# From its third chunk on, the first block in pairs of fp16 with scales from g_norm and the weights; the second block's weights kept in SBUF

## The chip, the cores and the metric

The kernel runs on one core of a Trainium2 chip. The metric is the time on the device in microseconds, from launch to end. Three runs of the kernel before gave 1608.7 us as their median (1608.4 to 1612.33).

## The reference, cut to what matters

```python
kv  = einsum('bhsd,bhse->bhde', k, v)           # linear attention, 8 x 8 heads, 576 tokens, 64 wide
out = einsum('bhsd,bhde->bhse', q, kv)
x   = out / sqrt(mean(out**2, -1) + 1e-6) * g_norm   # -> 4608 tokens x 512
h   = x @ moe_w_in                              # first block: 512 -> 2048
x   = maximum(0.01 * h, h) @ moe_w_out          # 2048 -> 512
h   = x @ moe2_w_in                             # second block: 512 -> 2048
P   = a[0] + a[1]*h + a[2]*h**2 + a[3]*h**3
Q   = 1 + |b[0]|*|h| + |b[1]|*h**2
out = (P / (Q + 1e-6)) @ moe2_w_out             # 2048 -> 512
```

The weights arrive as fp64 words; the kernel narrows them to fp32 itself.

## The kernel before

The 4608 tokens are 9 chunks of 512 columns; the hidden width of 2048 is 16 tiles f of 128. Each matrix product of a block is made from pairs, a high part and the rest, in three matmuls: `mm3` (L294) multiplies low weight by high value, high by high and high by low into one PSUM tile. A chunk and a tile f take 12 matmuls of 128x128 by 512 columns into ph (`emit_h`, L302: the weights W[0,f]) and 12 into the four y tiles (`emit_y`, L308: W[1,f]); so 384 a chunk and block.

In the first block the pairs are of fp32r: weights in W (pool wp, tile `w{part}_{f}`, 4 KB a partition for high and low), x in X (`new_x`), g in `new_g`. In the second block they are of fp16: `split16` (L285) multiplies by a power of two, ScalarE writes the high part, VectorE the rest. The powers come from measured sizes: largest weights (`wst`), largest x2 values (`xst`).

The first block goes by units (L801): unit 0 and 1 are tiles 0 to 5 of chunks 0 and 1 and run inside a startup whose order is written out by hand (`STARTUP`), unit 2 and 3 are tiles 6 to 15 of chunks 0 and 1, units 4 to 10 are all tiles of chunks 2 to 8. One f of a unit is a slot (`sl`). A slot issues, in this order: loads, the 12 matmuls into ph, "early" steps, leaky on ScalarE (L554), the high part of g on ScalarE (L841), the low part on VectorE (L234), the 12 matmuls into y of the tile two slots back (LAG = 2), "pe" and "post" steps, and then weight work. The slots also carry the next chunk's attention (`prep`, L703), to whose results `sx` (L764) gives the form of pairs. The y tiles of a chunk are read out by `evac_y` (L327) and stored to DRAM as x2; chunks 0 and 1 pass through yp, since they are added up in two halves.

Unit 2 converts the rest of w1 (CONVERT, L804): in slot s the narrowing of two tiles on VectorE (L263 to L273), gl, and the rests of W[0, 8+s] and W[1, 6+s]; both are read from two slots on. Units 4 to 9 narrow w2 (three tiles f a unit), measure it and store it in fp32 to DRAM (w2f). Unit 10, the last, loads it back (`load_w2`, L793) and splits it into fp16 (`split_w2`, L289). `w2s`, `w2next` and `rest` carry this over the border into the second block.

The second block takes two tiles f at once (j, 8 to a chunk); ScalarE and VectorE work out the rational function, GpSimd the low half of g. The scales of chunk 8 are asked for in its chunk 0, at j = 3, and worked out at j = 4 (L981 to L984); `x_scales_ask` sends sums through DRAM, `x_scales` (L196) is a chain of small operations on VectorE and ScalarE.

Each engine works in its own order, as the program issues it; TensorE's order is the one above. All loads and stores but a few are on SP's queue, in order.

Of the kernel before, what the change touches and what calls it, by code (L numbers as in the profile page):

```python
# [48 lines left out]
def kernel(  # L49
# [40 lines left out]
    w2f = [dp.tile([P, 2, NC * P], F32, tag=f"w2_{f}", name=f"w2_{f}") for f in range(NF)]  # L90
# [9 lines left out]
    small = const.tile([P, 25 + 23 * NCH], F32, name="small")  # L100
# [8 lines left out]
    wst, wq, aba, b0a, sw, nw = (part_of_small(*x) for x in ((2, NC), (2, NC), (4,), (1,), (2,), (2,)))  # L109
    xst, xq = part_of_small(NCH, NC), part_of_small(NCH, NC)  # L110
# [12 lines left out]
    def set_constants(spread):  # L123
        nc.vector.memset(ones.bitcast(F32), 0.0)
        nc.vector.memset(ones[0:D, 0:D].bitcast(F32), 1.0 / D)
        nc.vector.memset(ones[D:P, D:P].bitcast(F32), 1.0 / D)
# [54 lines left out]
    def weight_scales(t):  # L181

        reduce(nw[:, 0:1], t[:, 0, :], ALU.add)
        reduce(nw[:, 1:2], t[:, 1, :], ALU.max)
        over_root(sw, nw)
        nc.vector.scalar_tensor_tensor(out=nw, in0=nw, scalar=MS_R, in1=sw, op0=ALU.mult, op1=ALU.mult)
        pow2_below(sw, sw)
        nc.vector.tensor_scalar_mul(sw, sw, TOP * MS_R)

# [99 lines left out]
    def split_w2(f, part, src):  # L289
        t = wp.tile([P, 4, NC * P], F16, tag=f"w{part}_{f}", name=f"v{part}_{f}")  # L290
        W[part, f] = (t[:, 0, :], t[:, 1, :])
        split16(*W[part, f], src, sw[:, part:part + 1])
# [9 lines left out]
    def emit_h(f, dst, xs):  # L302
        wh, wl = W[0, f]
# [4 lines left out]
    def emit_y(f, ys, gh, gl, first, last):  # L308
        wh, wl = W[1, f]
        for e in range(NC):  # L310
            mm3(ys[e], wh[:, e * P:(e + 1) * P], wl[:, e * P:(e + 1) * P], gh, gl, first, last)
# [15 lines left out]
    def evac_y(ys, dst, engines=(nc.scalar, nc.vector), part=None, to=None, x=None, scale=None):  # L327

        for i in range(NC // 2):
            t = part[i] if part else raw() if to is None else to[:, 2 * i:2 * i + 2, :]  # L330
            for j in range(2):
                src = ys[2 * i + j]
                if part:
                    nc.vector.tensor_tensor(out=t[:, j, :], in0=src, in1=t[:, j, :], op=ALU.add)
                elif scale is not None:
                    nc.scalar.activation(out=t[:, j, :], in_=src, func=AF.Copy, scale=scale)
# [24 lines left out]

    def split_x(c, cc, src):
        if cc == 0:
            t = [xp.tile([P, 2, N], F16, tag=f"xh{i}", name=f"x16_{i}") for i in range(NC)]
            X[NCH + c] = [[x[:, i, :] for x in t] for i in range(2)]
        split16(X[NCH + c][0][cc], X[NCH + c][1][cc], src, col["sx"][:, c:c + 1])

    with tc.manual_schedule():
        Y = {}
        G = {}  # L370
        with ExitStack() as actx:
# [180 lines left out]
            def leaky(ps):  # L552
                t = scratch("t", 3, "t")
                nc.scalar.activation(out=t, in_=ps, func=AF.Prelu, alpha=0.01)  # L554
                return t
# [137 lines left out]
            STEPS = {"tl": p_table, "c": lambda: set_constants(spread), "g": lambda: load_gain(gsc_row), "cg": p_gain, "mc": make_constants, "wu": p_warm,  # L693
# [9 lines left out]
            def prep(c, po_at, ms_at, w_at, x_at, bursts, joint=False):  # L703
# [60 lines left out]
                def sx(p):  # L764
                    if p == 0:
                        X[c] = new_x()
# [26 lines left out]
            def load_w2(parts):  # L793
                t = raw()
                for i, (f, part) in enumerate(parts):
                    nc.sync.dma_start(out=t[:, i, :], in_=w2f[f][:, part, :])
                return t

# [9 lines left out]
            w2n, w2next = [], None  # L808
# [4 lines left out]
            for ui, (c, f0, f1) in enumerate(units):  # L813
# [11 lines left out]
                for f in range(f0, f1):  # L825
# [4 lines left out]
                    w2s = w2n  # L830
                    w2n = [x for x in ((f, 0), (f - LAG, 1)) if 0 <= x[0]] if last else []
                    w2raw, w2next = w2next, load_w2(w2n) if w2n else None
# [17 lines left out]
                    for _ in range({2: 0, 3: 2}.get(sl, 1) if joint else len(pend) > LAG):  # L850
# [4 lines left out]
                        if pf == p1 - 1:  # L855
                            evac_y(Y.pop(pc), yp[pc] if p1 < NF else x2[pc], part=parts, to=squares() if joint else None,
                                   x=pc if p1 == NF else None)
# [5 lines left out]
                    if 3 < ui and not last:  # L863
                        for _ in range(({3: 1, 4: 1, 8: 1, 9: 1, 11: 1, 13: 1} if joint else {3: 1, 4: 1, 6: 1, 8: 1, 10: 1, 12: 1}).get(sl, 0)):
                            if conv2:
                                t, ui_, part = conv2.pop(0)
                                narrow_abs([t], ui_)
                                narrow([t], ui_)
                                reduce(wq[:, part, :], ui_[:, 0, :].bitcast(F32).rearrange("p (c n) -> p c n", c=NC), ALU.max, True)
                                nc.vector.tensor_tensor(out=wst[:, part, :], in0=wst[:, part, :], in1=wq[:, part, :], op=ALU.max)  # L870
                                if not conv2:
                                    stores.append((w2f[wf], u.bitcast(F32)))
                        if sl in ((2, 6, 9) if joint else (2, 5, 8)) and todo:
                            wf = todo.pop()
                            u = cvp.tile([P, 2, N], U32, tag="cv", name="cv")
                            conv2 = [(load_w64(w2, wf, i, raw(1, I64)[:, 0, :]), u[:, i:i + 1, :], i) for i in range(2)]
                    if ui == len(units) - 2 and sl == 9:
                        asked = weight_scales_ask()
                    if ui == len(units) - 2 and sl == 11:
# [8 lines left out]
                    for i, (wf, part) in enumerate(w2s):  # L888
                        split_w2(wf, part, w2raw[:, i, :])
# [30 lines left out]
        rest = []  # L920

        def emit_y2():
# [3 lines left out]
            emit_y(pf, Y[pc], *pg, pf == p0, pf == p1 - 1)  # L926
# [3 lines left out]
            if pc < NCH:  # L930
                evac_y(ys, x2[pc], (nc.scalar, nc.scalar), x=pc)
            elif pc < 2 * NCH - 1:
                evac_y(ys, out[pc - NCH].rearrange("e p n -> p e n"), scale=col["y"][:, pc - NCH:pc - NCH + 1])
# [12 lines left out]
        for c in range(NCH):  # L946
            kc = NCH + c
            for j in range(NP):
                ph = ps_h2.tile([P, 2, N], F32, tag="h2", name="ph2")
                gt = new_g16()  # L950
                if c == NCH - 1 and j == NP - 1:
                    split(*prev)
                    done = None
                    for i in range(2):
                        if i:
                            ph = ps_h2.tile([P, 2, N], F32, tag="h2", name="ph2")
                        emit_h(2 * j + i, ph[:, i, :], X[kc])
# [5 lines left out]
                else:  # L963
                    for i in range(2):
                        emit_h(2 * j + i, ph[:, i, :], X[kc])
# [8 lines left out]
                for f, part, t in rest:  # L974
                    split_w2(f, part, t)
                rest = []
                if c == 0 and j < 2:
                    fs = w2n if j == 0 else [(NF - 2, 1), (NF - 1, 1)]
                    t = w2next if j == 0 else load_w2(fs)
                    rest = [(f, part, t[:, i, :]) for i, (f, part) in enumerate(fs)]  # L980
# [51 lines left out]
```

## Time and profile before

| | |
|---|---|
| runs, median | 1608.7 us (1608.4 to 1612.33) |
| profiled execution | 1609.07 us, of which the span in the trace is 1607.3 us |
| TensorE busy | 1596.7 us, 99% |
| VectorE busy | 978.3 us, 61% |
| ScalarE busy | 823.2 us, 51% |
| chain that ended last | TensorE 96%, DMA 2%, ScalarE 1% |

The profile is of one execution. Times in it are microseconds from the span's start unless marked ns; PE is TensorE's matmuls, PEld its weight loads (which overlap), DVE VectorE, ACT ScalarE, POOL GpSimd, SP the queue of transfers. Matmuls are pipelined: one lasts longer than the distance to the next, so their rate is read from what happens at equal places in a loop.

### The profile page before, as it was taken

The page shows a single profiled execution, that of the slowest core. Times are in us where ns is not written, and L with a number is a line of the kernel's source. Part 1 is how long each engine was busy: PE and PEld are TensorE (multiplying, and loading weights), DVE is VectorE, ACT ScalarE, POOL GpSimd, SP SyncE. Part 2 cuts the span into 40 slices and gives each one's busy share as a digit, 9 for nine tenths or more (in the row PEclk, how much of TensorE's full clock was granted, in tenths as well). Part 3 has the DMA queues.
Part 4 walks back from the last instruction along what each step waited for, and adds up shares of the span by engine and source line. Part 5 has one row for each costly group of instructions (what it writes and reads, how often), then busy time and mean ns, then how long its engine had stood idle before and what let it go on. Part 6 is the DMA issues. An engine that isn't in the chain of part 4 may idle for free.

```text
span 1607.3 us, 19258 instructions
## 1 busy us (share of the span) xinstructions
PE 1596.7 (99%) x7904; PEld 1020.5 (63%) x7904; DVE 978.3 (61%) x1240; ACT 823.2 (51%) x1074; POOL 151.9 (9%) x74
## 2 busy tenths in 40 slices
PE   8999999999999999999999999999999999999999
PEld 5888778888888888878885444444444444444444
DVE  6786244434454444442367877777777777777776
ACT  6554333323333232332366666666666666666665
POOL 0000000000000000000001222212222222112221
PEclk9999999999999999999999999999999999999999
DMA  8454634342434333121241010101000010101000
GB/s 315 125 182 150 174 103 132 94 143 72 139 94 129 119 92 109 42 85 30 87 162 66 2 53 0 53 0 44 10 27 27 4 49 1 53 0 53 1 27 27
DMA packets 45660, 123.61 MB, mean 77 GB/s; under 512 B 6148, under 2 KB 6660, under 8 KB 45572
## 3 DMA queue, kind: packets, MB, share of 16 engines
q1 hardware_dynamic: 43248, 118.06, 22.9%
q10 hardware_dynamic: 2324, 4.33, 1.1%
q8 instruction: 62, 1.02, 0.3%
q14 instruction: 26, 0.21, 0.0%
HBM read 90.90 MB, written 31.46 MB: 76 GB/s over the span
## 4 chain that ended last, share of the span: by engine, by line
PE 96%; DMA 2%; ACT 1%; DVE 0%; issue 0%; SPq 0%; DVEq 0%
PE ph L295 16%; PE y L297 16%; PE ph L297 16%; PE ph L296 16%; PE y L295 16%; PE y L296 16%; PE kvacc L406 1%; DMA raw<-in_kv_dram 1%; PE po L423 1%; PE pm L623 1%; DMA dqx<-small 0%; DMA raw<-dqx 0%; PE po L436 0%; ACT p L905 0%; ACT z L911 0%; PE bc L642 0%
## 5 line engine op out<-in xcount | busy, mean ns | idle before, releaser
L234 DVE TENSOR_TENSOR gl<-t,gh 128x512 fp32r<-128x512 f32 x144 | 99.4, 691 | 338.5 <-ACT gh L841 326.1
L234 POOL TENSOR_TENSOR gl<-p,gh 128x1024 f16<-128x1024 f32 x70 | 151.7, 2166 | 1431.8 <-PE y L297 865.1
L554 ACT ACTIVATE t<-ph 128x512 f32<-128x512 f32 x144 | 85.7, 595 | 353.3 <-PE ph L297 352.9
L295 PE MATMUL ph<-xh,w 128*128 128x512 f32 x576 | 226.8, 394 | 0.0
L295 PE MATMUL y<-gh,w 128*128 128x512 f32 x576 | 224.4, 390 | 0.0
L296 PE MATMUL ph<-xh,w 128*128 128x512 f32 x576 | 224.3, 389 | 0.0
L297 PE MATMUL ph<-xl,w 128*128 128x512 f32 x576 | 224.3, 389 | 0.0
L297 PE MATMUL y<-gl,w 128*128 128x512 f32 x576 | 224.2, 389 | 0.0
L296 PE MATMUL y<-gh,w 128*128 128x512 f32 x576 | 224.1, 389 | 0.0
L297 PE MATMUL y<-gl,v 128*128 128x512 f16 x576 | 218.3, 379 | 1.7 <-POOL gl L234 1.7
L295 PE MATMUL y<-gh,v 128*128 128x512 f16 x576 | 218.3, 379 | 0.3 <-ACT gh L239 0.3
L295 PE MATMUL ph<-x,v 128*128 128x512 f16 x576 | 218.3, 379 | 0.0
L296 PE MATMUL ph<-x,v 128*128 128x512 f16 x576 | 218.3, 379 | 0.0
L297 PE MATMUL ph<-x,v 128*128 128x512 f16 x576 | 218.3, 379 | 0.0
L296 PE MATMUL y<-gh,v 128*128 128x512 f16 x576 | 218.3, 379 | 0.0
L295 PEld LDWEIGHTS <-v 128*128 128x128 f16 x1152 | 112.7, 98 | 138.1 <-issue 2.5
L903 ACT ACTIVATE e<-ph,small 128x1024 f32<-128x1024 f32 (+1 forms) x73 | 80.3, 1101 | 233.0 <-PE ph L297 233.0
L296 PEld LDWEIGHTS <-v 128*128 128x128 f16 x1152 | 112.7, 98 | 136.1 <-issue 0.6
L297 PEld LDWEIGHTS <-v 128*128 128x128 f16 x1152 | 112.7, 98 | 135.9
L906 DVE SCALAR_TENSOR_TENSOR e<-s,b,e 128x1024 f32<-128x1024 f32 (+1 forms) x73 | 92.7, 1270 | 148.0 <-ACT s L904 148.0
L295 PEld LDWEIGHTS ph<-xh,w 128*128 128x128 f32 x576 | 108.1, 188 | 29.2 <-issue 4.7
L295 PEld LDWEIGHTS y<-gh,w 128*128 128x128 f32 x576 | 108.1, 188 | 23.1 <-ACT tmp L258 0.4
(139 smaller groups left out, 2059.9 us busy)
## 6 DMA issues: line engine op xcount, KB each, us to landing
raw<-in_kv_dram SPq DMA_DIRECT2D x33, 512.0 KB, 5.8
tmp<-in_w_dram SPq DMA_DIRECT2D x32, 512.0 KB, 7.1
raw<-in_w_dram SPq DMA_DIRECT2D x32, 512.0 KB, 5.6
raw<-x SPq DMA_DIRECT2D x18, 512.0 KB, 5.5
w<-cv SPq DMA_DIRECT2D x16, 512.0 KB, 2.9
raw<-w SPq DMA_DIRECT2D x32, 256.0 KB, 3.6
out_dram<-raw SPq DMA_DIRECT2D x16, 512.0 KB, 2.9
raw<-in_qT_dram SPq DMA_DIRECT2D x28, 256.0 KB, 4.7
```

The source lines that it names most:

```text
L234: (nc.gpsimd if pool else nc.vector).tensor_tensor(out=lo, in0=src, in1=hi if hi.dtype == F16 else hi.bitcast(F32), op=ALU.subtract)
L295: nc.tensor.matmul(out=dst, lhsT=wl, rhs=xh, start=first, stop=False, **kw)
L296: nc.tensor.matmul(out=dst, lhsT=wh, rhs=xh, start=False, stop=False, **kw)
L297: nc.tensor.matmul(out=dst, lhsT=wh, rhs=xl, start=False, stop=last, **kw)
L406: nc.tensor.matmul(out=acc[s * D:(s + 1) * D, k * D:(k + 1) * D], lhsT=t[:, 0, c], rhs=t[:, 1, c], start=first and k == 0, stop=last, skip ...
L423: nc.tensor.matmul(out=dst[s][j * D:(j + 1) * D, o], lhsT=KV[bt][r, 2 * g + j, :], rhs=q[r, j, o], start=True, stop=True)
L554: nc.scalar.activation(out=t, in_=ps, func=AF.Prelu, alpha=0.01)
L623: nc.tensor.matmul(out=dst[32 * p:32 * (p + 1)], lhsT=pick, rhs=x, start=True, stop=True)
L903: nc.scalar.activation(out=e, in_=ph, func=AF.Abs, scale=k["e"])
L906: nc.vector.scalar_tensor_tensor(out=e, in0=s, scalar=b1[:, 0:1], in1=e, op0=ALU.mult, op1=ALU.add)
```

## The change

- Chunks 2 to 8 of the first block use fp16 pairs. In slots 5 to 9 of unit 3 and 0 to 9 of unit 4, `narrower` rewrites the 32 fp32r weight pairs as fp16 pairs (one ScalarE pass, two VectorE passes each), half the size, into places freed by the tile before. x gets the scale sx1, g the scale sg1 (in leaky's activation), y the scale sy1 in `evac_y`.
- The scales come from g_norm (`gain_scales`, at the end of the startup, with `gn` made in `p_gain`), and from the largest weights: `first_weight_top` on each of the 32 high parts, one a slot in unit 2, up to six a slot in unit 3, slots 0 to 3. `first_weight_norms` follows at slot 3, at slot 4 a matmul with the all-ones matrix adds over the partitions, and `first_scales` works the scales out.
- w2 is narrowed into tiles of wp that are free (V, in units 5 to 8, four f a unit in place of three in units 4 to 9), not stored to DRAM, and split in the last unit from there (W2).
- `weight_scales_ask` moves from slot 9 to 10, `weight_scales` from 11 to 13. Chunk 8's `x_scales_ask` and `x_scales` move from j = 3 and 4 of the second block's chunk 0 to j = 3 and 6 of its chunk 1.

```diff
-    w2f = [dp.tile([P, 2, NC * P], F32, tag=f"w2_{f}", name=f"w2_{f}") for f in range(NF)]
...
+    def gain_scales():
+
+        nc.vector.tensor_scalar(out=pgain, in0=gn, scalar1=2.0 ** -40, scalar2=None, op0=ALU.max)
+        pow2_below(pgain, pgain)
+        nc.vector.tensor_copy(out=sx1, in_=pgain)
+        one_over(sx1)
+        nc.vector.tensor_scalar_mul(sx1, sx1, 2.0 ** 11)
+        nc.vector.memset(m1, 0.0)
+
+    def first_weight_top(f, part):
+        reduce(wq[:, part, :], W[part, f][0].bitcast(F32).rearrange("p (c n) -> p c n", c=NC), ALU.max, True)
+        nc.vector.tensor_tensor(out=m1[:, part, :], in0=m1[:, part, :], in1=wq[:, part, :], op=ALU.max)
+
+    def first_weight_norms():
+        nc.vector.tensor_scalar(out=m1[:, 0, :], in0=m1[:, 0, :], scalar1=pgain, scalar2=None, op0=ALU.mult)
+        nc.vector.tensor_tensor(out=m1, in0=m1, in1=m1, op=ALU.mult)
+        reduce(nw1, m1, ALU.add)
+
+    def first_scales(ps):
+
+        over_root(sw1, ps)
...
+        over_root(sg1, nw1[:, 0:1])
+        nc.scalar.activation(out=sg1, in_=sg1, func=AF.Square, scale=MS_R)
...
+    order1 = [(p, k) for k in range(NF // 2) for p in range(2)]
+    order2 = [(p, k) for k in range(NF // 2, NF) for p in range(2)]
+    new_tiles, V, W2 = {}, {}, {}
+
+    def narrower(f, part):
+
+        if f not in new_tiles:
+            if f:
+                p, k = order1[f - 1]
+                t = wp.tile([P, 4, NC * P], F16, tag=f"w{p}_{k}", name=f"n_{f}")
+                new_tiles[f] = t[:, 0:2, :], t[:, 2:4, :]
+            else:
+                new_tiles[f] = [xp.tile([P, 2, NC * P], F16, tag=f"xl{i}", name=f"n_0{i}") for i in range(2)]
+        (wh, wl), t, s = W[part, f], new_tiles[f][part], sv1[:, part:part + 1]
+        hi, lo = t[:, 0, :], t[:, 1, :]
+        nc.scalar.activation(out=hi, in_=wh.bitcast(F32), func=AF.Copy, scale=s)
+        nc.vector.scalar_tensor_tensor(out=lo, in0=wh.bitcast(F32), scalar=s, in1=hi, op0=ALU.mult, op1=ALU.subtract)
+        nc.vector.scalar_tensor_tensor(out=lo, in0=wl.bitcast(F32), scalar=s, in1=lo, op0=ALU.mult, op1=ALU.add)
+        W[part, f] = hi, lo
...
+                nc.scalar.activation(out=gn, in_=t[:, 0:1], func=AF.Abs)
...
-                    split(X[c][0][p], X[c][1][p], x)
+                    split16(X[c][0][p], X[c][1][p], x, sx1)
...
-                        G[c, f // 2] = new_g()
+                        G[c, f // 2] = new_g16() if c > 1 else new_g()
...
-                    t = leaky(ph)
+                    t = leaky(ph, sg1) if c > 1 else leaky(ph)
...
+                    for _ in range(1 if ui == 2 else 6 if ui == 3 else 0):
+                        if top_of:
+                            first_weight_top(*top_of.pop(0))
+                    if ui == 3 and sl == 3:
+                        assert not top_of
+                        first_weight_norms()
+                    if ui == 3 and sl == 4:
+                        norms = bank("h", "norms")
+                        nc.tensor.matmul(out=norms[:, 0:2], lhsT=ones.bitcast(F32), rhs=nw1, start=True, stop=True)
+                        first_scales(norms[:, 0:2])
+                    for _ in range((3 if sl in (6, 7) else 2) if ui == 3 and sl > 4 else 2 if ui == 4 else 0):
+                        if wide and (ui > 3 or wide[0][0] < HALF):
+                            narrower(*wide.pop(0))
-                    if 3 < ui and not last:
...
+                    if 4 < ui and not last:
+                        if conv2 and sl in (3, 4, 7, 8, 11, 12, 14, 15):
...
-                            u = cvp.tile([P, 2, N], U32, tag="cv", name="cv")
...
+                            u = V[wf] = wp.tile([P, 2, N], U32, tag=home2(wf), name=f"u_{wf}")
...
-                if c == 0 and j == 3:
+                if c == 1 and j == 3:
                     asked = x_scales_ask(NCH - 1, 1)
-                if c == 0 and j == 4:
+                if c == 1 and j == 6:
                     x_scales(asked, NCH - 1, 1)
```

## Rows read from the trace of the kernel before

**Rows 1.** The page's head, busy time by engine, and the chain that ended last.
```profile
span 1607.3 us, 19258 instructions
...
PE 1596.7 (99%) x7904; PEld 1020.5 (63%) x7904; DVE 978.3 (61%) x1240; ACT 823.2 (51%) x1074; POOL 151.9 (9%) x74
...
PE 96%; DMA 2%; ACT 1%; DVE 0%; issue 0%; SPq 0%; DVEq 0%
```
**Rows 2.** Windows: stretch, busy us per engine, granted clock: units 2, 3, 4; second block.
```profile
90.00:145.00 55.00, 55.00 (x245) 45.53 (x244) 53.70 (x88) 32.57 (x56) 0.00 (x0) 1.00 0.51 162
145.00:209.00 64.00, 64.00 (x440) 50.39 (x439) 18.49 (x26) 21.28 (x36) 0.00 (x0) 1.00 0.54 154
209.00:301.00 92.00, 92.00 (x498) 74.06 (x497) 39.85 (x67) 30.91 (x52) 0.00 (x0) 1.00 0.39 118
1140.00:1540.00 400.00, 400.00 (x1855) 181.36 (x1854) 296.33 (x252) 264.78 (x271) 81.50 (x38) 1.00 0.07 24
```
**Rows 3.** Order of time, ScalarE, first block: start, duration, instruction, [idle before].
```profile
300.37 0.60 ACT L554 ACTIVATE t<-ph 128x512 f32<-128x512 f32 x1 [4.18 <-PE ph L297]
...
311.25 0.60 ACT L554 ACTIVATE t<-ph 128x512 f32<-128x512 f32 x1 [4.18 <-PE ph L297]
```
**Rows 4.** Order of time, SP's queue, second block.
```profile
953.01 1.54 SPq L324 DMA_DIRECT2D out_dram<-raw  x2
...
1533.16 1.54 SPq L324 DMA_DIRECT2D out_dram<-raw  x2
```
**Rows 5.** Groups by line and form: weight loads of either block.
```profile
L296 PEld LDWEIGHTS <-v 128*128 128x128 f16 x1152 | 112.7, 98 | 136.1 <-issue 0.6
L296 PEld LDWEIGHTS ph<-xh,w 128*128 128x128 f32 x576 | 108.2, 188 | 21.7
```
**Rows 6.** Order of time, VectorE, unit 2.
```profile
96.73 0.69 DVE L263 TENSOR_SCALAR tmp<-tmp 128x1024 f32<-128x1024 f32 x1 [0.24 <-ACT tmp L258]
...
103.61 0.68 DVE L263 TENSOR_SCALAR tmp<-tmp 128x1024 f32<-128x1024 f32 x1
...
136.99 1.28 DVE L234 TENSOR_TENSOR w<-cv,w 128x512 fp32r<-128x512 f32 x2
138.29 0.69 DVE L263 TENSOR_SCALAR tmp<-tmp 128x1024 f32<-128x1024 f32 x1
```
**Rows 7.** Order of time, TensorE, start of unit 2's slot 9.
```profile
139.30 0.39 PE L295 MATMUL ph<-xh,w 128*128 128x512 f32 x1
```
**Rows 8.** Order of time, VectorE: w2's sizes in unit 5, a split in the second block.
```profile
326.26 0.69 DVE L155 TENSOR_REDUCE small<-cv 128x4 f32<-128x512 f32 x1
326.98 0.16 DVE L870 TENSOR_TENSOR small<-small 128x4 f32<-128x4 f32 x1
...
882.32 1.41 DVE L287 SCALAR_TENSOR_TENSOR v<-raw,small,v 128x512 f16<-128x512 f32 x2
```
**Rows 9.** Order of time, VectorE and TensorE: unit 3, start of unit 4.
```profile
162.06 1.29 DVE L334 TENSOR_TENSOR raw<-y,raw 128x512 f32<-128x512 f32 x2 [2.86 <-DMA raw<-yp]
...
177.77 1.06 PE L623 MATMUL pm<-sq,pick 128*32 128x512 f32 x8
...
180.32 0.50 PE L295 MATMUL ph<-xh,w 128*128 128x512 f32 x1
...
206.44 0.69 DVE L234 TENSOR_TENSOR xl<-o,xh 128x512 fp32r<-128x512 f32 x1 [0.70 <-ACT xh L239]
...
209.12 0.39 PE L295 MATMUL ph<-xh,w 128*128 128x512 f32 x1
```
**Rows 10.** Order of time, VectorE and TensorE: second block, chunk 0.
```profile
903.21 0.29 DVE L155 TENSOR_REDUCE small<-raw 128x1 f32<-128x128 f32 x1 [1.77 <-DMA raw<-dqx]
...
912.43 0.38 PE L295 MATMUL y<-gh,v 128*128 128x512 f16 x1 [0.30 <-ACT gh L239]
...
914.70 0.38 PE L297 MATMUL y<-gl,v 128*128 128x512 f16 x1 [1.67 <-POOL gl L234]
```

More of the change, by code (lines that the diff above doesn't have):

```diff
@@ L99 @@
     lnb = const.tile([P, 3], F32, name="lnb")
-    small = const.tile([P, 25 + 23 * NCH], F32, name="small")
+    small = const.tile([P, 49 + 23 * NCH], F32, name="small")
     at = [0]
@@ L109 @@
     wst, wq, aba, b0a, sw, nw = (part_of_small(*x) for x in ((2, NC), (2, NC), (4,), (1,), (2,), (2,)))
+    sx1, sg1, sy1 = (part_of_small(1) for _ in range(3))
+    pgain, m1, sw1, nw1 = part_of_small(1), part_of_small(2, NC), part_of_small(2), part_of_small(2)
+    sv1 = part_of_small(2)
+    gn = part_of_small(1)
     xst, xq = part_of_small(NCH, NC), part_of_small(NCH, NC)
@@ L306, in emit_h, with emit_y @@
                 cc == 0, cc == NC - 1)
-    def emit_y(f, ys, gh, gl, first, last):
-        wh, wl = W[1, f]
+    def emit_y(f, ys, gh, gl, first, last, w=W):
+        wh, wl = w[1, f]
         for e in range(NC):
@@ L334, in evac_y @@
                     nc.vector.tensor_tensor(out=t[:, j, :], in0=src, in1=t[:, j, :], op=ALU.add)
+                elif scale is not None and engines[j] is nc.scalar:
+                    nc.scalar.activation(out=t[:, j, :], in_=src, func=AF.Copy, scale=scale)
                 elif scale is not None:
-                    nc.scalar.activation(out=t[:, j, :], in_=src, func=AF.Copy, scale=scale)
+                    nc.vector.tensor_scalar_mul(t[:, j, :], src, scale)
                 elif engines[j] is nc.scalar:
@@ L550, in bank, with leaky @@
                 return (ps_h if at == "h" else ps_a if at == "att" else ps_y).tile([P, N], F32, tag=at, name=name)
-            def leaky(ps):
+            def leaky(ps, scale=1.0):
                 t = scratch("t", 3, "t")
-                nc.scalar.activation(out=t, in_=ps, func=AF.Prelu, alpha=0.01)
+                nc.scalar.activation(out=t, in_=ps, func=AF.Prelu, alpha=0.01, scale=scale)
                 return t
@@ L807 @@
             todo = list(range(NF))[::-1]
-            w2n, w2next = [], None
+            wide = [(f, part) for f in range(NF) for part in range(2)]
+            top_of = [(f, part) for f in range(NF) for part in range(2)]
             parts = None
@@ L862 @@
                         parts = load_pairs(yp[units[ui - 1][0]])
-                    if 3 < ui and not last:
[L864 to L873, printed above, removed]
+                    for _ in range(1 if ui == 2 else 6 if ui == 3 else 0):
+                        if top_of:
+                            first_weight_top(*top_of.pop(0))
@@ new lines @@
+                    if 4 < ui and not last:
+                        if conv2 and sl in (3, 4, 7, 8, 11, 12, 14, 15):
+                            t, ui_, part = conv2.pop(0)
+                            narrow_abs([t], ui_)
+                            narrow([t], ui_)
+                            reduce(wq[:, part, :], ui_[:, 0, :].bitcast(F32).rearrange("p (c n) -> p c n", c=NC), ALU.max, True)
+                            nc.vector.tensor_tensor(out=wst[:, part, :], in0=wst[:, part, :], in1=wq[:, part, :], op=ALU.max)
+                        if sl in (2, 6, 9, 12) and todo:
@@ L874 @@
                             wf = todo.pop()
-                            u = cvp.tile([P, 2, N], U32, tag="cv", name="cv")
-                            conv2 = [(load_w64(w2, wf, i, raw(1, I64)[:, 0, :]), u[:, i:i + 1, :], i) for i in range(2)]
-                    if ui == len(units) - 2 and sl == 9:
+                            u = V[wf] = wp.tile([P, 2, N], U32, tag=home2(wf), name=f"u_{wf}")
+                            conv2 += [(load_w64(w2, wf, i, raw(1, I64)[:, 0, :]), u[:, i:i + 1, :], i) for i in range(2)]
@@ L878 @@
+                    if ui == len(units) - 2 and sl == 10:
                         asked = weight_scales_ask()
-                    if ui == len(units) - 2 and sl == 11:
+                    if ui == len(units) - 2 and sl == 13:
                         weight_scales(asked)
@@ L887 @@
                         split_x(0, sl - 8, xr[sl - 8])
-                    for i, (wf, part) in enumerate(w2s):
-                        split_w2(wf, part, w2raw[:, i, :])
+                    if last:
+                        for part in range(2):
+                            split_w2(f, part)
                 if f1 == NF:
```

72 lines of the change are left out of this document (37 added, 35 removed).

## The prediction

> **What bounds the kernel now.** I read the page first. TensorE is busy 99% of the span and holds 96% of the chain that ended last [rows 1], and the windows show the granted clock at 1.00 throughout, the level of 2.4 GHz [rows 2]. So the time is the number of matmuls times their spacing, plus the few places where TensorE waits. A busy TensorE says nothing about the spacing, so the next view is order of time. In a stretch of the first block without attention work, the leaky activations of three slots begin at 300.37 and 311.25 us [rows 3]: 10.88 us for 2 x 24 matmuls, 226.7 ns each. In the second block a chunk's outputs are stored at 953.01 and, seven chunks later, at 1533.16 us [rows 4]: 82.88 us for 384 matmuls, 215.8 ns each. Same columns, same clock, 10.9 ns apart. What differs is the type: the first block's weights load in 188 ns each, the second's in 98 ns [rows 5].
>
> The third view is VectorE by stage. It is nearly full only in unit 2, where w1's last tiles are converted: 53.70 of 55 us. In unit 3 it has 45 of 64 us free, in unit 4 52 of 92 [rows 2]. The change puts its new work into exactly these units, so the question is what VectorE's order does there.
>
> **The matmuls.** Units 4 to 10 (chunks 2 to 8) have 7 x 384 = 2688 block matmuls, which become the form that the second block already runs. At 226.7 - 215.8 = 10.9 ns each [rows 3, 4] this is **29.2 us less**. Attention's own matmuls keep their type. The Trainium skill (TensorE: Matmul & The Clock Gate, Back-to-back issue gap) gives an isolated gap of N / 2.4 + 2.5 ns, which for 512 columns is 215.8 ns, and its formula names no type; by it both blocks would run alike and this term would be zero. The second block agrees with it, the first block's 226.7 ns does not, so the measurement decides. The sum here goes by the rows alone.
>
> **Unit 2 (one weight tile's size per slot).** The steady part runs from the narrowing at 103.61 us to that at 138.29 us: six slots in 34.68 us, 5.78 us of VectorE per slot [rows 6], against 24 x 226.7 ns = 5.44 us of TensorE. VectorE is thus falling behind already, by 0.34 us a slot, and lives on a lead. The lead is spent last at slot 7: the low half of W[0,15] begins at 136.99 and takes 0.69, so it is there at 137.68 us, and the matmul that reads it starts at 139.30 us [rows 6, 7]. 1.62 us are left.
>
> The change adds before that point:
> - `gain_scales`, seven small VectorE operations in front of unit 2's first narrowing. Small operations that follow each other start about 0.2 us apart (the maximum takes 0.16 us [rows 8]), and the memset less: 1.1 us, of which 0.24 us fall into an idle stretch at 96.73 us [rows 6]. Bounds 0.7 and 1.5.
> - seven times a reduction and a maximum (slots 0 to 6). The trace has the same pair for w2: the reduction begins at 326.26, the maximum at 326.98 us [rows 8], and the next independent operation follows some 0.08 us after so small a one. So 0.80 us each, 5.6 us; bounds 0.69 and 0.9 each, 4.8 and 6.3.
>
> 1.1 - 0.24 + 5.6 = 6.46 us of new work against 1.62 us of lead: TensorE waits 4.8 us, in pieces, at the starts of slots 5 to 9, and with a hand-over at each **5.0 us more**. The bounds give 3.5 to 6.5. Queued behind the conversion are the low halves of g; they have two slots' time and are not late before the weights are.
>
> **Unit 3 (22 more sizes, the norms, 12 conversions).** Everything in it moves back by the 5 us. VectorE comes out of unit 2 at about 153.6 us (the last narrowing at 138.29 and its slot of 5.78 end at 144.1, plus gl, ten pairs and 0.9 of gain_scales). Slots 0 to 3 then hold 22 x 0.80 = 17.6 us, four gl of 0.6 and the two additions of unit 2's stored part. Of the latter the second waits for its transfer, in the trace until 162.06 us [rows 9], so until 167 us now, and its reduction ends near 169.5. From there: 4.8 (slot 1), 5.4, 3.8 and 0.5 for the norms make 184.0 us. TensorE reaches the norms' matmul where slot 5 began, at 180.32 us [rows 9], plus 5.0: 185.3 us. I take no wait, with 1.3 us to spare, and **0.5 us** for the matmul itself (eight of pm, of 512 columns, take 1.06 us [rows 9]; bounds 0.2 and 1.0). If pairs cost 0.9 us, the 22 use that spare time up and TensorE waits 0 to 1 us.
>
> Behind it stand `first_scales` (about 14 small operations that cross to ScalarE and back, some 4 us) and 12 conversions. A conversion is one ScalarE pass and two VectorE passes. The nearest, L287, does two in 1.41 us [rows 8], so 1.4 us; bounds 1.3 and 1.75 (if each waits for the one before it). Slots 5 to 7 take 2, 3, 3: VectorE enters slot 8 some 2.6 us later against TensorE than now, the two conversions of slot 8 come ahead of X[2]'s last two pieces and cost 2.8 more: 5.4 us. X[2]'s last piece was ready at 207.13 us (begun at 206.44), and it is read as the eleventh or twelfth matmul after 209.12 us [rows 9], near 211.6: 4.5 us of cover. So the first matmuls of chunk 2 wait **0.9 us**; bounds 0 and 4.
>
> **Units 4 to 10 and the second block.** In unit 4 two conversions a slot replace w2's narrowing: 2.8 + 0.6 us of VectorE in slots of 5.2, with six slots' lead before each tile is read. In units 5 to 8 eight w2 conversions of 3.2 us each stand where six did; the unit of 93 us is under half full. In unit 10 the split reads SBUF where it read a transferred buffer; same two passes. The 16 stores and 32 loads that go were on SP and nobody on TensorE's path waited for them: zero. If that cover were gone, w2's splitting would wait on one 256 KB load. ScalarE's scaled Prelu and the scaled eviction cost at most 0.1 us each, in slots where it is a third busy: zero.
>
> The last piece is chunk 8's x_scales, now in chunk 0 of the second block. VectorE waits 1.77 us there for its sums, until 903.21 us, and ScalarE stands behind it in the same chain; what they deliver late is GpSimd's low half of g, and TensorE waits 0.30 us on gh and 1.67 us on gl [rows 10]. The two matmuls between those waits, 0.43 us apart in a regular stream, lie 2.27 us apart, so 1.84 + 0.30, about 2.2 us are lost. With three groups between asking and using, in chunk 1, the sums have long landed. That takes the 1.77 us out of the delay; the chain of small operations stays, and the rest of the loss, 0.4 us, with it: **1.8 us less**, bounds 0 and 2.2.
>
> **The sum**, against the profiled execution's own 1609.07 us (span 1607.3 [rows 1]; 0.4 us above the median of the runs): 1609.07 - 29.2 + 5.0 + 0.5 + 0.9 - 1.8 = **1584.5 us**. With all the terms at their low ends (3.5, 0.2, 0, -2.2) it is 1581.4, at their high ends (6.5, 1.0, 4, 0) 1591.4.
>
> **The rivals.**
> - *The backlog is hidden.* If the pairs slip into gaps, only the matmuls, norms and x_scales count: 1609.07 - 29.2 + 0.5 - 1.8 = 1578.6 us. For it: VectorE has 45 us free in unit 3. Against: none of it lies in unit 2.
> - *VectorE binds through units 2 and 3.* If pairs cost 0.9 and conversions 1.75 us, 32 x 0.1 + 12 x 0.35 = 7.4 us more stand in a queue whose spare time I have counted as used up but for 1.3: 1584.5 + 6 = 1590.5 us. For it: every new operation reads what its neighbour wrote. Against: the same kinds run at the shorter spacing today.
> - *The spacing is the stage's, not the type's* (the other side). Then the matmuls keep 226.7 ns and only the costs stay: 1609.07 + 6.4 - 1.8 = 1613.7 us, slower. It decides from 1.7 ns a matmul (4.6 us over 2688): if the spacing falls by less, the change loses. The page's formula would end here, in that it ties no part of the gap to the type. Against it: the first block keeps 226.7 ns in unit 4, where VectorE is 43% busy, and the second has 215.8 ns at 74% [rows 2].
> - *Part of the change does nothing:* keeping w2 in SBUF, and x_scales' move if its ping-pong still delays the pool. 1586.3 us, inside the range.
>
> **How the numbers follow.** Mine 0.59 (the last rival's case included), hidden 0.17, VectorE bound 0.20, spacing of the stage 0.04. The likeliest gives 1584.5, its own range 1581 to 1589; with the two neighbours 1577.5 to 1591, which leaves out little more than the fourth. A difference under 0.3% (4.8 us) can't be told from none; the fourth case lies at +0.29% and is shared between same and slower. Faster 0.95, same 0.02, slower 0.03.
>
> **What would show it.** Spacing of 215.8 ns in units 4 to 10 (a slot of 5.18 us without attention). TensorE waiting for VectorE's weight tiles at the starts of slots 5 to 9 of unit 2, about 5 us together, and unit 3 starting that much later. No wait at the norms' matmul, and a short one at chunk 2's first matmuls. No wait of 1.67 us on the pool near the second block's fifth group, a smaller one a chunk later at most. I am wrong if slots of chunk 3 on take over 5.3 us, if unit 2 shows no wait, or if TensorE waits in unit 4 for converted tiles.

## The result, and the profile after

The changed kernel took 1591.26 us in the median (1587.38 to 1592.11, 4 runs), the kernel before 1609.79 us (1608.4 to 1612.33, 4 runs): a ratio of 0.9878 [0.9856, 0.99]. That is 18.5 us less, where the prediction had 24.6 us against the profiled execution; the median lies 0.3 us above the upper end of the range (1591), and the difference of 18.5 us just inside it (1609.07 - 1591 is 18.1 us).

The profiled execution of after took 1592.08 us. Its page, head, chain and clock:

```profile
span 1590.3 us, 19302 instructions
...
PE 1575.1 (99%) x7906; PEld 782.9 (49%) x7906; DVE 1052.4 (66%) x1389; ACT 856.3 (54%) x1110; POOL 150.3 (9%) x74
...
PEclk8999999999999999999999999999999999999999
...
PE 91%; DVE 5%; DMA 2%; ACT 2%; issue 0%; SPq 0%; DVEq 0%
```

Beside [rows 1], TensorE is as full as before, but 5% of the chain is now VectorE's; the long stretch of it lies in unit 2, from 93.73 to 147.99 us, and ends so:

```profile
147.38 0.61 DVE w L271
148.00 0.04 issue
148.04 0.50 PE ph L359
```

The weight loads, which overlap the matmuls, fell by 238 us of busy time, the span by 17.

To place the difference I took the start of equal matmuls in both traces, after minus before, from front to end:

| place | offset, us | step, us |
|---|---|---|
| start of unit 2 | +4.62 | +4.6 |
| end of unit 2 | +8.91 | +4.3 |
| behind the norms' matmul | +9.15 | +0.25 |
| second slot of unit 4 | +15.15 | +6.0 |
| end of unit 10 | -14.81 | -30.0 |
| end | -16.95 | -2.1 |

**The matmuls.** After's ScalarE in unit 5, order of time (start, duration, instruction, [idle before]), answers to [rows 3]:

```profile
374.01 0.69 ACT L623 ACTIVATE t<-ph,small 128x512 f32<-128x512 f32 x1 [3.83 <-PE ph L361]
...
379.19 0.69 ACT L623 ACTIVATE t<-ph,small 128x512 f32<-128x512 f32 x1 [0.18 <-PE ph L361]
```

One slot of 24 matmuls is 5.18 us, 215.8 ns each. The store queue in the second block, as in [rows 4], shows that block unchanged but for its first chunks: the seven chunks between the two stores below take 82.94 us each, where [rows 4] gave 82.88.

```profile
935.61 1.55 SPq L388 DMA_DIRECT2D out_dram<-raw  x2
...
1516.22 1.54 SPq L388 DMA_DIRECT2D out_dram<-raw  x2
```

**Unit 2.** TensorE's matmuls that waited, in order of time:

```profile
109.11 0.50 PE L359 MATMUL y<-gh,w 128*128 128x512 f32 x1 [0.39 <-ACT raw L404]
...
128.64 0.50 PE L359 MATMUL ph<-xh,w 128*128 128x512 f32 x1 [0.18 <-DVE w L271]
...
135.10 0.50 PE L359 MATMUL ph<-xh,w 128*128 128x512 f32 x1 [0.69 <-DVE w L271]
...
141.57 0.50 PE L359 MATMUL ph<-xh,w 128*128 128x512 f32 x1 [0.69 <-DVE w L271]
...
148.04 0.50 PE L359 MATMUL ph<-xh,w 128*128 128x512 f32 x1 [0.69 <-DVE w L271]
```

Slots 6 to 9 begin 6.46 us apart, each waiting for the weight tile that VectorE is just finishing; [rows 6] had 5.78 us of VectorE a slot. A wait's number in brackets is less than the time lost, since the matmul ahead of it runs out as well: by equal matmuls slots 5 to 9 lost 0.35, 1.02, 1.03, 1.03 and 0.17 us, and slot 2 another 0.7 us.

**Unit 4's start.** TensorE, then ScalarE and VectorE:

```profile
218.28 0.39 PE L359 MATMUL ph<-x,n 128*128 128x512 f16 x1
...
222.52 0.38 PE L359 MATMUL ph<-x,n 128*128 128x512 f16 x1 [2.77 <-ACT x L323]
...
223.31 0.38 PE L361 MATMUL ph<-x,n 128*128 128x512 f16 x1 [0.20 <-DVE x L324]
...
224.66 0.45 PE L359 MATMUL ph<-x,n 128*128 128x512 f16 x1 [0.98 <-ACT x L323]
...
229.72 0.39 PE L359 MATMUL ph<-x,n 128*128 128x512 f16 x1
```
```profile
207.35 0.37 ACT L480 COPY kv<-kvacc 128x256 f32<-128x256 f32 x1 [2.69 <-PE kvacc L475]
207.62 1.95 ACT L341 ACTIVATE n<-w,small 128x512 f16<-128x512 f32 x3
```
```profile
208.38 0.75 DVE L342 SCALAR_TENSOR_TENSOR n<-w,small,n 128x512 f16<-128x512 f32 x1 [3.00 <-ACT n L341]
```

A slot of 5.18 us takes 11.44 us. Read from the end: the matmuls wait for pieces of x; ahead of those, VectorE stood idle for 3.00 us until 208.38, for the high halves of slot 7's three conversions; and ScalarE could not write these, because they stand in its order behind the copy of kv's accumulator, which waited 2.69 us for TensorE. The windows (TensorE alone: busy, granted clock in the third column from the end) show what followed:

```profile
219.00:223.00 4.00, 1.23 (x6) 1.00 0.00 0
223.00:225.00 2.00, 0.83 (x4) 0.96 0.00 0
225.00:227.00 2.00, 2.00 (x6) 0.50 0.00 0
227.00:229.00 2.00, 2.00 (x7) 0.69 0.00 0
```

After 1.23 us of work in 4 us the clock fell to 0.50, the level of 1.2 GHz, with all pieces there. About 4.4 us of the slot's loss are waits and 1.6 us clock.

**The startup** was not in the sum. Windows of 20 to 30 us (busy time of PE, PEld, DVE, ACT, POOL, then the granted clock), before and after:

```profile
20.00:30.00 10.00, 10.00 (x105) 4.91 (x101) 9.52 (x18) 7.94 (x15) 0.00 (x0) 1.00 1.02 398
```
```profile
20.00:30.00 10.00, 10.00 (x86) 5.33 (x84) 6.16 (x10) 3.87 (x9) 0.00 (x0) 0.50 1.03 402
```

Half the clock for 10 us, and unit 2 begins at 94.96 instead of 90.34 us. What the change puts ahead of this stretch is small: the matrix of ones is written in one piece where there were three, and `p_gain` has one activation more.

### The profile page after: what moved, and what is told of

It is laid out like the page before. It is cut to its first block, busy times and chain, and to the rows that moved or that the text cites. A ratio compares the mean times of both kernels' runs of the same rounds, so it can differ in the third digit from the quotient of the medians.

```text
span 1590.3 us, 19302 instructions
## 1 busy us (share of the span) xinstructions
PE 1575.1 (99%) x7906; PEld 782.9 (49%) x7906; DVE 1052.4 (66%) x1389; ACT 856.3 (54%) x1110; POOL 150.3 (9%) x74
## 3 DMA queue, kind: packets, MB, share of 16 engines
q8 instruction: 62, 1.02, 0.3%
## 4 chain that ended last, share of the span: by engine, by line
PE 91%; DVE 5%; DMA 2%; ACT 2%; issue 0%; SPq 0%; DVEq 0%
PE ph L359 15%; PE ph L361 15%; PE ph L360 15%; PE y L361 15%; PE y L359 15%; PE y L360 15%; PE kvacc L475 1%; DMA raw<-in_kv_dram 1%; PE po L492 1%; DVE w L271 1%; PE pm L693 1%; DMA dqx<-small 1%; DVE tmp L306 0%; DVE gl L271 0%; DVE tmp L310 0%; DVE small L156 0%
## 5 line engine op out<-in xcount | busy, mean ns | idle before, releaser
L271 DVE TENSOR_TENSOR gl<-t,gh 128x512 f16<-128x512 f32 (+1 forms) x144 | 99.6, 691 | 237.8 <-ACT gh L901 225.5
L623 ACT ACTIVATE t<-ph,small 128x512 f32<-128x512 f32 x112 | 76.7, 685 | 253.2 <-PE ph L361 249.4
L359 PE MATMUL ph<-x,n 128*128 128x512 f16 x448 | 170.0, 380 | 4.3 <-ACT x L323 3.8
L361 PE MATMUL ph<-x,n 128*128 128x512 f16 x448 | 170.0, 379 | 0.2 <-DVE x L324 0.2
L360 PE MATMUL ph<-x,n 128*128 128x512 f16 x448 | 170.0, 380 | 0.0
L359 PE MATMUL y<-gh,n 128*128 128x512 f16 x448 | 169.8, 379 | 0.0
L360 PE MATMUL y<-gh,n 128*128 128x512 f16 x448 | 169.8, 379 | 0.0
L361 PE MATMUL y<-gl,n 128*128 128x512 f16 x448 | 169.8, 379 | 0.0
L359 PEld LDWEIGHTS <-n 128*128 128x128 f16 x896 | 87.6, 98 | 108.8 <-issue 4.5
L360 PEld LDWEIGHTS <-n 128*128 128x128 f16 x896 | 87.7, 98 | 108.6 <-issue 5.1
```

The source lines that it names most:

```text
L271: (nc.gpsimd if pool else nc.vector).tensor_tensor(out=lo, in0=src, in1=hi if hi.dtype == F16 else hi.bitcast(F32), op=ALU.subtract)
L359: nc.tensor.matmul(out=dst, lhsT=wl, rhs=xh, start=first, stop=False, **kw)
L360: nc.tensor.matmul(out=dst, lhsT=wh, rhs=xh, start=False, stop=False, **kw)
L361: nc.tensor.matmul(out=dst, lhsT=wh, rhs=xl, start=False, stop=last, **kw)
```

## The experiments

e_before, e_memset, e_late and e_notop2 ran on one chip, e_warm, e_order, e_xs and e_best on another; the kernel before took 1614.81 us on the first (1611.44 to 1619.17, 17 runs) and 1609.24 us on the second (1608.29 to 1616.3, 9 runs). Ratios are to these. Where two versions differ by less than a few us, I go by equal places in their traces, since the startup's clock differs between executions.

### The startup's clock: chance or change?

**e_before** is the kernel before, run again. **e_memset** is the changed kernel with its matrix of ones made in three writes, as many as before:

```diff
-        nc.vector.memset(ones.bitcast(F32), 1.0)
+        nc.vector.memset(ones.bitcast(F32), 0.0)
+        nc.vector.memset(ones[0:D, 0:P].bitcast(F32), 1.0)
+        nc.vector.memset(ones[D:P, 0:P].bitcast(F32), 1.0)
```

> The kernel before, unchanged, run again to see the granted clock of several executions. Theory A (the half clock between 20 and 30 us, which the changed kernel's profile shows and which cost 4.95 us there, comes by chance into any execution of either kernel): one or two executions of five show a mean clock of 0.996 or 0.997 and lie some 3 to 5 us above the others; the rest show 0.999. Theory B (the change brings it, because the all-ones matrix is ready 0.35 us sooner and the warm matmuls begin sooner): all five show 0.998 or 0.999 and lie within 1.5 us.

> The changed kernel with the all-ones matrix written by three memsets, as before the change, in place of one. Theory B (the change's single memset starts the warm matmuls 0.35 us sooner, and so brings the half clock from 20 us on): the warm matmuls begin at 1.40 us again, the clock stays at 1.00 until unit 4 in all executions, the time falls by about 4 us to 1587. Theory A (chance): the executions are divided as the changed kernel's are, some with 0.998, some with 0.995 to 0.997, and the median is within 2 us of it.

e_before: 1614.86 us (1611.89 to 1618.8, 12 runs), ratio 1.0004 [0.9992, 1.0015]. Its profiled execution has the fall, with not one instruction changed:

```profile
20.00:30.00 10.00, 10.00 (x84) 4.94 (x80) 5.66 (x9) 3.63 (x8) 0.00 (x0) 0.51 1.02 400
```

Unit 2 starts 4.3 us later in it than in the first trace of the same kernel. Seven of its 12 executions have a mean clock of 0.995 or 0.996 and 1614.78 to 1618.8 us, five 0.999 or 1.0 and 1611.89 to 1613.95 us. e_memset took 1592.15 us (1589.03 to 1594.72, 4 runs), ratio 0.9863 [0.9847, 0.9879], and its profiled execution still fell to 0.50, from 20.6 to 30.8 us. So the fall needs nothing of the change: it comes and goes in the kernel before too, and costs 4 to 5 us where it comes. By the mean clock (0.997 or less) it came in up to 18 of 38 executions of the kernel before on these two chips; 13 of them have 0.996 or less. The other five, at 0.997, may owe it to shorter falls elsewhere: e_notop2's profiled execution has 0.997 too, with 1.00 from 20 to 30 us.

**e_warm** is the changed kernel with six more of the startup's warm-up matmuls in the order written out by hand:

```diff
- ... oc,0,0,w0_10 km,1,0 nw,0 ...
+ ... oc,0,0,w0_10 wu,6 km,1,0 nw,0 ...
```

> The changed kernel with six more warm matmuls in the startup, in the 1.7 to 2.4 us in which TensorE waits for kv's second load just before the clock falls. Theory: the half clock from 20 us on follows this idle stretch, and where it comes is chance; with the stretch filled, all executions show 1.00 between 20 and 30 us, mean clock 0.998, and lie within 1.5 us of each other near the fastest of the changed kernel on this chip, about 1589 us. Rival (the fall has to do with the light work before, the thin matmuls of po, pm and kv, and not with the idle stretch): the executions stay divided, some at 0.994 to 0.996 and 4 us longer.

1588.91 us (1587.78 to 1590.49, 4 runs), ratio 0.9863 [0.9839, 0.9886]. TensorE is busy for 9.39 of the 10 us ahead of the stretch, where it was busy for 7.78 in after, and then:

```profile
20.00:30.00 10.00, 10.00 (x126) 4.94 (x124) 9.43 (x17) 8.02 (x16) 0.00 (x0) 1.00 1.03 402
```

All four have a mean clock of 0.998 or 0.999, though their times lie 2.7 us apart and not within 1.5; with the last kernel below, which has the same six, none of nine fell to 0.997. The profiled one fell elsewhere: half clock from 11.2 to 14.6 us. So its 9.39 us are not the fill's alone, since at half clock TensorE is busy longer with the same matmuls (0.43 us from one to the next where e_xs's clock falls, 0.22 before); e_notop2, without the fill, has that early fall too, 9.86 us of work from 10 to 20 us, and 1.00 from 20 to 30. The clean case is e_best: the fill, no early fall, 9.64 us of work, and 1.00 from 20 to 30 us. But e_xs stays at 1.00 after 8.52 us without any fill. That the fill prevents the fall is thus supported by 0 of 9 against 13 to 18 of 38, but no single trace shows it; what decides it from one execution to the next is not known.

### Unit 4's start: the conversions ahead of x

**e_late** takes the conversions of slots 7 to 9 of unit 3 out, so that slot 5 has two, slot 6 three, and the rest come two a slot in unit 4:

```diff
-for _ in range((3 if sl in (6, 7) else 2) if ui == 3 and sl > 4 else 2 if ui == 4 else 0):
+for _ in range({5: 2, 6: 3}.get(sl, 0) if ui == 3 else 2 if ui == 4 else 0):
```

> The changed kernel with the seven conversions of unit 3's slots 7 to 9 moved into unit 4 (5 in unit 3, 27 in unit 4, still two a slot). Theory: they stand ahead of chunk 2's x in VectorE's and ScalarE's order, and cost 6.0 us at the start of unit 4, waits of 2.8, 0.2 and 1.0 us and the half clock that follows. Then those waits go, the clock stays at 1.00 through unit 4's first slots, and the time falls by 5 to 6 us; unit 4 gains no wait, since each tile is still ready two slots before it is read. Rival (x is late for its own chain: the multiplication, the high part and the rest cross between the engines four times): the wait stays at 3 us or more and the time falls by less than 3 us.

1585.44 us (1585.09 to 1589.82, 5 runs), ratio 0.9828 [0.9813, 0.9843]. TensorE does not wait at unit 4's start and keeps its clock:

```profile
214.00:224.00 10.00, 10.00 (x46) 6.98 (x46) 6.08 (x9) 6.93 (x11) 0.00 (x0) 1.00 0.01 2
```

By equal matmuls the slot is 6.1 us shorter than in after: the whole 6.0 us come from where these seven conversions stand, clock included. The medians differ by 6.7 us from e_memset's (the same chip), the faster executions of either (mean clock 0.998 there, 0.999 or more here) by about 4.5.

**e_order** leaves the number of conversions and moves only slot 7's three, ahead of the "post" steps, that is ahead of the copy of kv's accumulator:

```diff
+if ui == 3 and sl == 7:
+    for _ in range(3):
+        narrower(*wide.pop(0))
...
-for _ in range((3 if sl in (6, 7) else 2) if ui == 3 and sl > 4 else 2 if ui == 4 else 0):
+for _ in range({5: 2, 6: 3, 8: 2, 9: 2}.get(sl, 0) if ui == 3 else 2 if ui == 4 else 0):
```

> The changed kernel with the three conversions of unit 3's slot 7 issued before that slot's attention steps, not behind them; nothing is taken out. Theory: in ScalarE's order the copy of kv's accumulator stands ahead of them and waits for TensorE until the slot's end, so their first VectorE pass began 3.0 us late, and all that follows with it, x included. Then VectorE's idle 3.0 us go, chunk 2's x is ready 3 us sooner, TensorE's wait at unit 4's start falls from 4.0 us to 1 to 2 us, the half clock behind it does not come, and the time falls by 4 to 5 us. Rival (the number of conversions alone makes x late, wherever they stand): the wait stays above 3 us.

1588.94 us (1583.98 to 1591.6, 4 runs), ratio 0.9858 [0.9831, 0.9886]. VectorE and TensorE:

```profile
204.75 0.75 DVE L342 SCALAR_TENSOR_TENSOR n<-w,small,n 128x512 f16<-128x512 f32 x1
...
211.04 0.69 DVE L838 TENSOR_TENSOR o<-o,sq 128x512 f32<-128x512 f32 x1 [1.85 <-DMA sq<-rs]
```
```profile
220.83 0.38 PE L359 MATMUL ph<-x,n 128*128 128x512 f16 x1 [1.65 <-ACT x L323]
```

The 3.00 us of idle VectorE are gone: the queue on ScalarE was their cause. But the gain came through only in part. VectorE now waits 1.85 us for the row norms' transfer, x is multiplied from 211.04 instead of 212.74 us, and the first wait is 1.65 rather than 2.77 us. The slot's waits in brackets add up to 2.8 us where after has 4.0; I had expected 1 to 2. The half clock came all the same and lasted 6.8 us (from 222.0 us) where after has 3.4 (from 224.8), so this slot lost 5.96 us as before. What holds x's last two pieces back are slot 8's two conversions, ahead of them on VectorE from 216.43 to 219.34 us; with these out as well, as in e_late and in e_best below, which keeps slot 9's, x is in time.

### Unit 2: the sizes on VectorE

**e_notop2** has no sizes in unit 2; it leaves out the sizes of tiles 0 to 4, so the first block's scales come from the other 22:

```diff
-            top_of = [(f, part) for f in range(NF) for part in range(2)]
+            top_of = [(f, part) for f in range(5, NF) for part in range(2)]
...
-                    for _ in range(1 if ui == 2 else 6 if ui == 3 else 0):
+                    for _ in range(6 if ui == 3 else 0):
```

> The changed kernel without the ten sizes of unit 2: the largest weights are taken over 22 of the 32 tiles only. Theory: those reductions use up VectorE's lead in unit 2 and cost TensorE 4.3 us at the starts of slots 5 to 9. Then the five waits go and the time falls by 4.3 us; what remains of gain_scales (1.0 us against a lead of 1.6) shows no wait. Rival (the lead is lost to gain_scales, or the waits come back in unit 3, at the norms or at chunk 2's x): the time falls by less than 2 us.

1585.48 us (1584.98 to 1586.61, 4 runs), ratio 0.9823 [0.9811, 0.9836]. TensorE waits nowhere in unit 2, so `gain_scales` by itself stays inside the lead. One loss is new, 0.6 us at unit 3's slot 2, where chunk 0's stored part now lands later against TensorE:

```profile
164.74 0.50 PE L359 MATMUL y<-gh,w 128*128 128x512 f32 x1 [0.31 <-DVE raw L398]
```

Net, 3.7 us by equal matmuls. The rest of the median's 6.7 us against e_memset is not unit 2's: this kernel's profiled execution has 1.00 from 20 to 30 us, where e_memset's is at half clock, and a shorter fall from 10.7 to 14.1 us.

### The second block's scales

**e_xs** puts chunk 8's scales back to where they were:

```diff
-                if c == 1 and j == 3:
+                if c == 0 and j == 3:
                     asked = x_scales_ask(NCH - 1, 1)
-                if c == 1 and j == 6:
+                if c == 0 and j == 4:
                     x_scales(asked, NCH - 1, 1)
```

> The changed kernel with chunk 8's scales asked for and worked out where they were before, in chunk 0 of the second block, groups 3 and 4. Theory: the move is worth what the trace of before lost there, 2.2 us, less the 0.45 us still lost in chunk 1. Then waits of 0.3 us on gh and 1.7 us on gl come back in chunk 0, the 0.45 us in chunk 1 go, and the second block takes 1.8 us longer. Rival (earlier stores or the shorter first block have changed where the sums land, so the old place would be as good): no wait on gl above 0.5 us.

One execution, 1590.76 us. Both waits of [rows 10] are back:

```profile
892.47 0.38 PE L359 MATMUL y<-gh,v 128*128 128x512 f16 x1 [0.30 <-ACT gh L276]
...
894.74 0.38 PE L361 MATMUL y<-gl,v 128*128 128x512 f16 x1 [1.68 <-POOL gl L271]
```

In after one of 0.29 us is left, a chunk later:

```profile
1001.35 0.38 PE L361 MATMUL y<-gl,v 128*128 128x512 f16 x1 [0.29 <-POOL gl L271]
```

By equal matmuls the second block is 3.5 us longer than in after with the old place, not the 1.8 us that I expected: the waits make 1.84 us of it, and half clock from 895.4 to 898.9 us, right behind the second wait, 1.7 us more. The first trace of the kernel before has the same two waits and stays at 1.00; e_before's has them (the one on gh 1.41 us there) and falls from 921.4 to 924.8 us. So the clock falls behind these waits in some traces and not in others, and the old place costs 1.84 us, or 1.7 us more than that.

### All of it together

**e_best** puts every repair into one kernel: the six warm matmuls; all sizes in unit 3, the norms at its slot 5 and their matmul at slot 6; three conversions ahead of the "post" steps of unit 3's slot 7, two in its slot 9, and two a slot in unit 4; the last unit's x_scales and split of x one slot later; chunk 8's scales at j = 7.

```diff
+ ... wu,6 ...
...
+if ui == 3 and sl == 7:
+    for _ in range(3):
+        narrower(*wide.pop(0))
...
-for _ in range(1 if ui == 2 else 6 if ui == 3 else 0):
+for _ in range({0: 6, 1: 3, 2: 6, 3: 6, 4: 6, 5: 5}.get(sl, 0) if ui == 3 else 0):
...
-if ui == 3 and sl == 3:
+if ui == 3 and sl == 5:
...
-if ui == 3 and sl == 4:
+if ui == 3 and sl == 6:
...
-for _ in range((3 if sl in (6, 7) else 2) if ui == 3 and sl > 4 else 2 if ui == 4 else 0):
+for _ in range({9: 2}.get(sl, 0) if ui == 3 else 2 if ui == 4 else 0):
...
-if last and sl == 6:
+if last and sl == 7:
...
-if c == 1 and j == 6:
+if c == 1 and j == 7:
```

> All that the runs point to together: six warm matmuls more in the startup; no size in unit 2, all 32 in slots 0 to 5 of unit 3, the norms two slots later; three conversions in slot 7 ahead of the attention steps, two in slot 9, the rest in unit 4; the last unit's scales used one slot later, chunk 8's scales at group 7 of chunk 1. Theory: each wait has its own cause, so they add up: 4.3 us (unit 2), 6.0 us (unit 4's start), 0.7 to 2.1 us (last unit), 0.45 us (second block), and the startup's 4.5 us in those executions that have it: about 1579 us on this chip against 1589 to 1594 for the changed kernel. Rival (what leaves unit 2 comes back as a wait at the norms or at chunk 2's x): above 1584 us.

1577.02 us (1576.01 to 1578.35, 5 runs), ratio 0.9789 [0.9766, 0.9811] to the kernel before: faster than that and than every other version of the changed kernel. From its page, and its waits on TensorE from 60 us on (us in total, times, longest):

```profile
PE 1568.8 (100%) x7912; PEld 781.0 (50%) x7912; DVE 1052.5 (67%) x1389; ACT 856.0 (54%) x1110; POOL 150.4 (10%) x74
```
```profile
PE y L359 <- DVE raw L398: 0.2, 1, 0.2
```

VectorE has exactly after's work, 1052.5 us against 1052.4. Nothing was made cheaper; it was only put where TensorE does not wait for it, and what is left of the time is matmuls. By equal matmuls it gains 15.05 us on after's profiled execution: 4.1 in the startup, 4.3 in unit 2 (0.5 of it lost again in unit 3), 6.1 at unit 4's start, 0.7 in the last unit and 0.45 in the second block.

## Why the prediction was right, and where it was not

| step | predicted, us | measured, us |
|---|---|---|
| matmuls of chunks 2 to 8 | -29.2 | -30.8 |
| unit 2 | +5.0 | +4.3 |
| norms' matmul | +0.5 | +0.25 |
| chunk 2's first matmuls | +0.9 | +6.0 |
| last unit | 0 | +0.55 |
| chunk 8's scales | -1.8 | -1.85 |
| startup's clock | not in the sum | +4.6 |

The measured steps add up to -16.95 us, as the traces do. 0.3 us of the matmuls' step lie behind the end of unit 10, where chunk 8's last 24 matmuls into y run among the second block's first ones.

**The matmuls: right.** From unit 4's second slot to the end of unit 10, 111 slots, the offset falls by 29.96 us, and 0.55 us of the last unit stand against it. In 93 of these slots it falls by 0.26 us, 10.8 ns for each of 24 matmuls, which is the sum's figure. The 1.6 us beyond the sum are not in the spacing: in fifteen slots the offset falls by 0.38 to 0.40 us, fourteen of them where block matmuls follow attention's. There the first distance is 0.34 us in the kernel before (in unit 4 from 221.12 us) and 0.23 in after (the same place, from 236.20 us), where the next ones are 0.227 and 0.216. The spacing went with the type, in the same units with the same columns and clock, so the rival in which it is the stage's is out. By the Trainium skill (TensorE: Matmul & The Clock Gate, Back-to-back issue gap) the formula for the isolated gap gives 215.8 ns for 512 columns and names no type; the traces here show it for fp16 alone. Why an fp32r pair costs more is not shown; that its loads took 188 ns [rows 5] is no more than what goes with it.

**Unit 2: right in place and mechanism, 0.7 us too much.** TensorE waits for weight tiles at the starts of slots 5 to 9, and e_notop2, without the sizes, has none of these waits. They cost 3.6 of the 5.0 us; the 0.7 us at slot 2 is a wait I did not name (y's bank, copied by ScalarE). A pair of reduction and maximum takes the 0.80 us of the price:

```profile
148.50 0.68 DVE L156 TENSOR_REDUCE small<-w 128x4 f32<-128x512 f32 x1
149.22 0.17 DVE L202 TENSOR_TENSOR small<-small 128x4 f32<-128x4 f32 x1
149.30 0.69 DVE L300 TENSOR_SCALAR tmp<-tmp 128x1024 f32<-128x1024 f32 x1
```

But VectorE's slot grew by 0.68 only (5.78 to 6.46 us): the old slot held some 0.1 us that was not work (34.13 of 34.68 us busy over the six slots of [rows 6]). Seven times that is 0.7 us, half of the 1.4 us by which these waits fell short of 5.0; where the rest went is not shown. The rival in which the backlog is hidden fell with the waits of unit 2.

**Norms: right.** There is no wait: VectorE was ready at 187.5 us, TensorE reached the matmul at 189.23.

**"So the first matmuls of chunk 2 wait 0.9 us; bounds 0 and 4": this step failed.** I counted VectorE's work (5.4 us) against the cover (4.5 us), each conversion at 1.4 us with its high half always there. Two things were missing. The conversions cross ScalarE, and there slot 7's stand behind a copy that waits for TensorE; the 3.00 us that VectorE lost to this are as large as most of the miss in waits (4.4 against 0.9). Yet they do not carry it alone: e_order, which removes just them, shortens the first wait by 1.1 us only, since the next late things, the norms' transfer and the conversions after it, take over. Then the clock, which no term had: after 1.23 us of work in 4 us it fell to half, 1.6 us more. The waits alone passed my upper bound of 4. e_late shows that all 6 us hang on where the conversions of slots 7 to 9 stand. The prediction asked what is queued behind the conversions on VectorE; it did not ask what stands ahead of them on ScalarE.

**The last unit: taken as zero, 0.55 us.** The fp16 slots are shorter (two in 10.36 us instead of 10.88), while the chain of x_scales between asking in slot 4 and using in slot 6 is as long as before; the leaky of slot 7 stands behind it on ScalarE, and one matmul, slot 9's first, waits:

```profile
798.44 0.38 PE L359 MATMUL ph<-x,n 128*128 128x512 f16 x1 [0.52 <-ACT t L623]
```

Five slots, from 4 to 9, last 25.9 us without a wait (e_best) where they lasted 27.2, so the cover is 1.3 us less. The size of the wait is chance: the sums land at another time in each trace. The kernel before shows none in its first trace and 1.0 us in e_before; the changed kernel with the split in its place shows it in all seven traces, 0.2 to 2.0 us. A faster unit takes cover away from a chain whose lead is counted in slots; how much of the 0.55 us is the change's, one pair of traces can't say.

**Chunk 8's scales: right**, 1.85 us between the traces of before and after, and 1.84 us of waits in e_xs. Where half clock follows the waits, as in e_xs, the old place costs 1.7 us more; no term had that.

**The startup** lies outside the sum, and it moves the median: without its 4.6 us the profiled execution would have been at 1587.5 us, and the one run of after whose mean clock (0.998) has no room for this fall took 1587.38 us. That is 2.9 us over the forecast, less than the miss at unit 4 alone.

The rival of a VectorE that binds through units 2 and 3 gave 1590.5 us, close to the result but by another way: that is luck. Pairs cost 0.80 and not 0.9 us, a conversion's two VectorE passes 1.45 and not 1.75 us (they begin at 208.38, 209.84 and 211.29 us), and VectorE's 3.00 us of idle time ahead of unit 4 are no part of that rival.

## What to carry to other kernels

When work that crosses two engines is added ahead of a tile that TensorE waits for, look in both engines' orders for what stands ahead of it and itself waits for TensorE; the sum of busy times does not show that. When a stage gets shorter, recount each lead that is given in slots: five slots of cover were 27.2 us and are now 25.9. And move work out of the stage whose lead is spent before trying to make it cheaper: here the same 1052 us of VectorE in other places, with the startup's idle stretch filled, brought the ratio from 0.988 to 0.979.

## What the runs showed of the hardware that was not expected

- The same program has two startups. In one trace of the kernel before TensorE's granted clock is 0.50 (1.2 GHz) from 20 to 30 us, after 10 us of which it was busy for 7.88; in another it stays at 1.00 after 7.98. On one chip, seven of twelve executions have a mean clock of 0.996 or less and five 0.999 or more. The difference is 4 to 5 us of 1610, as large as a real change of 0.3%.
- A wait in mid-kernel can cost more than itself: 4.4 us of waiting at unit 4's start were followed by half clock, 1.6 us more, and the same is seen in e_order, where e_late without the wait stays at 1.00. Waits of 0.3 and 1.7 us in the second block were followed by 3.4 us of half clock in e_xs and by none in the first trace of the kernel before.
- Matmuls of fp32r pairs run 226.7 ns apart and those of fp16 pairs 215.8, at the same clock and columns, though each load (188 and 98 ns) is shorter than either spacing. Behind attention's matmuls the first distance is 0.34 us for fp32r and 0.23 for fp16.
